# GpSimd's SBUF-only instructions made to wait for VectorE's in the attention of an attention, MoE and MLP kernel

## The chip, the cores and the metric

One core of a Trainium2 chip runs the whole program in one launch. The metric is the device time of that core in microseconds (us), the median of three runs. PE is TensorE (PEld its weight loads), DVE VectorE, ACT ScalarE, POOL GpSimd, SP SyncE. Each engine works through its own list of instructions in order; an instruction may wait on semaphores that others raise, and then everything behind it on its engine waits too.

## The reference

Three stages follow each other. Only the first is touched.

```python
q_pool = q.reshape(B, H, S // 2, 2, D).mean(axis=3)            # B, H, S, D = 4, 8, 1152, 64
scores = (1 / np.sqrt(D)) * (q_pool @ k.transpose(0, 1, 3, 2)) # 576 queries x 1152 keys a head
attn = np.exp(scores - scores.max(-1, keepdims=True))
x = (attn / (attn.sum(-1, keepdims=True) + 1e-9)) @ v          # -> 2304 tokens x 512
x = moe(x)                            # top-1 of 8 experts, 512 -> 1024 -> 512, gated
out = relu(x @ w_in) ** 2 @ w_out     # 512 -> 2048 -> 512
```

## The kernel before, in words

The 32 heads are worked off as 16 pairs, 18 steps a pair. In a step one tile of 128 keys x 512 queries goes through: PE makes the scores `st` (L397), ACT the exponential `p` in f32 (L415), whose upper half read as bf16 is the high part of the probability; the low part `pl` = `p` - high, f16, is made by `low` (L425); PE then multiplies both parts with the values (`pv`, L462). Three tiles a pair (`p32x`, `plx`) hold the odd queries. `low` goes to VectorE for the tiles in the plan's list `low` (every second one) and to GpSimd for the rest and for the odd tiles.

For the pair after that, the same steps carry the preparation: `prep` loads keys, queries and values and splits them in two f16 parts (`split`: ACT makes the high part, L239, VectorE the low one, L241; the outputs are `krow`, `qr2` and `vx`), GpSimd adds neighbouring queries (`qsum`, L261, output `qs`), which ACT then splits first; transposing DMAs turn them. The running maximum of the scores is found ahead of time in `smax_red`: ACT's `rd` from one PSUM tile (L364), then VectorE's fused maximum over another PSUM tile and `rd` (L367, with a short read of the accumulator behind it), block maxima `mc` (L358), and a small `tensor_scalar` from the maxima `mx` into `qr2` (L376). `kdiff` (L318) makes differences of keys on VectorE. `evac` scales the outputs out of PSUM (L484 to L503). `Route` classes the tokens of a finished batch between the steps; its `lo` (L691) makes `xhl`.

What stands where is set by `run`: each job has a step and a rank in it, and the lists of all engines are written in that order (ranks: load 0, scores 1, exponential 2, `smax_red` 2.2, 4.6 and 6.5, `kdiff` 4.4, `prep` 5, `low` 6, route 7). The schedule is manual: the order written is the order run, and semaphores are added only where data or a buffer calls for one. A VectorE instruction here is called **SBUF-only** when all it reads and writes lies in SBUF; L367, L358 and the evacuations read PSUM.

Of the kernel before, what the change touches and what calls it, by code (L numbers as in the profile page):

```python
# [14 lines left out]
ALU = mybir.AluOpType  # L15
# [121 lines left out]
class Attention:  # L137
# [3 lines left out]
    def __init__(self, ctx, kctx, pctx, tc, q, k, v, xbp, xdone):  # L141
        self.tc, self.nc = tc, tc.nc
        self.q, self.k, self.v = q, k, v
        self.xdone = xdone
        B, H, S, D = q.shape
        assert S == 1152 and D == 64
        self.B, self.H = B, H
        self.HP = H // 2
        self.NP = B * self.HP
        pool = lambda n, b, **kw: ctx.enter_context(tc.tile_pool(name=n, bufs=b, **kw))  # L150
        keys = lambda n, b: kctx.enter_context(tc.tile_pool(name=n, bufs=b, side="right"))
        self.raw = keys("raw", 1)
        self.row = keys("row", 1)
        self.t1p = keys("t1", 3)
        self.r2p = pool("r2", 2)
        self.pp = pool("pp", 22)
        self.sm = pool("sm", 2)
        self.xbp = xbp
        self.per = pool("per", 1)
        psum = lambda n, b: pctx.enter_context(tc.tile_pool(name=n, bufs=b, space=PSUM))  # L160
        self.ps_t = psum("ps_t", 2)
        self.ps_m = psum("ps_m", 4)
        self.ps_v = psum("ps_v", 2)
        self.t2 = [self.per.tile([128, 18, 128], F16, name=f"t2_{i}") for i in range(2)]
        self.qr2 = [self.per.tile([128, 9, 128], F16, name=f"qr2_{i}") for i in range(2)]
        self.vx = [self.per.tile([128, 18, 130], F16, name=f"vx_{i}") for i in range(2)]
        self.st = {}
        self.routes = {}

    def init(self):  # L170
        V = self.nc.gpsimd
        for t in self.qr2[::-1]:
            V.memset(t, 0.0)
        for t in self.vx:
            V.memset(t[:, :, 64:65], 1.0)
        for t in self.t2:
            V.memset(t[64:65], MROW)

        zero = self.qr2[1].rearrange("p a b -> p (a b)")[:, 0:512]
        ps = self.ps_m.tile([128, 512], F32, tag="sm", name="warm")  # L180
        for _ in range(WARM):
            self.nc.tensor.matmul(
                out=ps, lhsT=zero[:, 0:128], rhs=zero, start=True, stop=True,
                skip_group_check=True,
            )

    def load(self, h):
# [37 lines left out]
    def prep(self, h, n):  # L225
        nc = self.nc
        s = self.st[h]
        if n == 0:
            s["krow"] = self.row.tile([128, 18, 128], F16, tag="krow", name="krow")
            s["qrow"] = self.row.tile([128, 9, 128], F16, tag="qrow", name="qrow")  # L230
            s["qs"] = self.row.tile([128, 9, 64], F32, tag="qs", name="qs")
            s["t1"] = self.t1p.tile([128, 18, 128], F16, tag="t1", name="t1")
            s["r1"] = self.t1p.tile([128, 9, 128], F16, tag="r1", name="r1")
            s["qr2"] = self.qr2[h % 2]
            s["vx"] = self.vx[h % 2]

        def split(src, hi, lo, sc, what):
            if what == 0:
                nc.scalar.activation(out=hi, in_=src, func=ACTF.Copy, scale=sc)  # L239
            else:  # L240
                nc.vector.scalar_tensor_tensor(  # L241
                    out=lo, in0=src, scalar=sc, in1=hi, op0=ALU.mult, op1=ALU.subtract
                )

        def k_(i, what):
            kr = s["kr"][:, i].rearrange("p (c d) -> p c d", d=64)
            row = s["krow"][:, 9 * i:9 * i + 9]
            split(kr, row[:, :, 64:128], row[:, :, 0:64], KS, what)

        def v_(i, what):  # L250
            vr = s["vr"][:, i].rearrange("p (c d) -> p c d", d=64)
            vx = s["vx"][:, 9 * i:9 * i + 9]
            split(vr, vx[:, :, 0:64], vx[:, :, 65:129], VS, what)

        def kt(c=slice(0, 18)):
            nc.sync.dma_start_transpose(
                out=s["t1"][:, c], in_=s["krow"][:, c].rearrange("p a b -> p (a b)")
            )

        def qsum(c=slice(0, 9)):  # L260
            (nc.gpsimd if h else nc.vector).tensor_tensor(  # L261
                out=s["qs"][:, c], in0=s["qr"][:, c, 0], in1=s["qr"][:, c, 1], op=ALU.add
            )

        def q_(what, c=slice(0, 9)):
            split(s["qs"][:, c], s["qrow"][:, c, 0:64], s["qr2"][:, c, 0:64], QS, what)

        def qdup(c=slice(0, 9)):
            hi, dup = s["qrow"][:, c, 0:64], s["qrow"][:, c, 64:128]
            if h:  # L270
                nc.scalar.activation(out=dup, in_=hi, func=ACTF.Copy)
            else:
                nc.vector.tensor_copy(out=dup, in_=hi)
            nc.sync.dma_start_transpose(
                out=s["r1"][:, c], in_=s["qrow"][:, c].rearrange("p a b -> p (a b)")
            )

        if not h and n < 7:

            c, k = (slice(0, 4), slice(0, 9)) if n < 4 else (slice(4, 9), slice(9, 18))  # L280
            if n == 6:
                q_(1)
            elif n % 4 == 0:
                qsum(c)
                q_(0, c)
                k_(n // 4, 0)
            elif n % 4 == 1:
                qdup(c)
                k_(n // 4, 1)
                kt(k)  # L290
            return
        [
            lambda: (qsum(), k_(0, 0)),
            lambda: k_(0, 1),
            lambda: k_(1, 0),
            lambda: (k_(1, 1), kt()),
            lambda: q_(0),
            lambda: qdup(),
            lambda: q_(1),
            lambda: v_(0, 0),  # L300
            lambda: v_(0, 1),
            lambda: v_(1, 0),
            lambda: v_(1, 1),
        ][n]()
# [7 lines left out]
    def kdiff(self, h, a=slice(0, 2)):  # L312

        s = self.st[h]
        if a.start == 0:
            s["kd"] = self.sm.tile([128, 2, 512], BF16, tag="m24", name="kd")
        t1 = s["t1"].rearrange("p (a c) b -> p a (c b)", a=2)
        self.nc.vector.tensor_tensor(  # L318
            out=s["kd"][:, a], in0=t1[:, a, 512:1024], in1=t1[:, a, 0:512], op=ALU.subtract
        )  # L320

    def smax(self, h, i):

# [96 lines left out]
    def low(self, h, i, dve):  # L420
        nc = self.nc
        s = self.st[h]
        eng = nc.vector if dve else nc.gpsimd
        pl = s["pl", i] = self.ptile(i, "pl", F16)
        eng.tensor_tensor(out=pl, in0=s.pop(("p32", i)), in1=s["ph", i], op=ALU.subtract)  # L425

    GROUPS = (
        ((0, 0), (0, 1), (0, 2)),
# [1127 lines left out]
class First:  # L1556
# [97 lines left out]
    def psum(self, t, f2):  # L1654
        ps = self.att.ps_m.tile([128, 512], F32, tag="sm", name="h0")
        self.h[t, f2] = ps[:, 0:2 * T].rearrange("p (a b) -> p a b", a=2)
        return self.h[t, f2]
# [45 lines left out]
def build(tc, q, k, v, emb, tau, w1, w2, w_in, w_out, consts, at, out):  # L1703
    nc = tc.nc
    pool = lambda c, n, b, **kw: c.enter_context(tc.tile_pool(name=n, bufs=b, **kw))
    with ExitStack() as ctx, tc.manual_schedule():
# [3 lines left out]
        with ExitStack() as actx:  # L1710
# [18 lines left out]
            att = Attention(actx, kctx, pctx, tc, q, k, v, xbp, xdone)  # L1729
            first = First(moe, att)  # L1730
            init, zeros = moe.init(rb), moe.zeros()
            last = 18 * (att.NP - 1)
            extra = [(i, lambda: next(init, None)) for i in PLAN["init"]]
            extra += [(i, lambda: next(zeros, None)) for i in PLAN["zeros"]]

# [139 lines left out]
```

## Time and profile before

| | us |
|---|---|
| median of three runs (1138.07 to 1147.18) | 1143.66 |
| the profiled execution's own time | 1142.18 |
| its span, first to last instruction | 1140.4 |
| mean granted clock of TensorE, as a share of 2.4 GHz | 0.967 |
| busy: PE, DVE, ACT, POOL | 1061.1, 722.1, 527.5, 531.3 |

The attention takes the first 450 us or so of the span. A busy PE in such a profile has modelled ends, so 93% busy is not 93% of its peak. A group's row gives count, busy time, mean duration in ns, and the engine's idle time just before its instructions with what ended it.

### The profile page before, as it was taken

Reading aid. Unit: us, or ns where it says so; the run is one execution under the profiler, and the core shown is the slowest. Engines: PE = TensorE matmul, PEld = TensorE weight load, DVE = VectorE, ACT = ScalarE, POOL = GpSimd, SP = SyncE. Lnnn points to the kernel's source line nnn. Section 1 sums busy time; section 2 is a strip of 40 time slices with the busy share of each in tenths; the row PEclk is TensorE's granted clock in tenths of the full one; section 3 lists DMA queues with packets and bytes.
Section 4 is the critical chain, followed back from the end, with each engine's and each line's share of the span. In section 5 each row is a group of like instructions: output and inputs, shape, how many; then the busy total and the mean of one; then the engine's idle time right before and its main releaser. Section 6 shows DMA issues by size and latency. Waiting matters only on the chain. (4 is left out here: it accounts for less than half of the span.)

```text
span 1140.4 us, 28256 instructions
## 1 busy us (share of the span) xinstructions
PE 1061.1 (93%) x11340; PEld 724.6 (64%) x11340; DVE 722.1 (63%) x1374; ACT 527.5 (46%) x998; POOL 531.3 (47%) x454
## 2 busy tenths in 40 slices
PE   6898899999999889999899799998799999999996
PEld 2465556656665566999899699975454454555543
DVE  6999989999998988866664548848850021211200
ACT  5776677678876756423222335534440031322200
POOL 4765655566765646522443426637760142322301
PEclk9999989999998989999999899999899999999998
DMA  8665765656766537569579699223310000000000
GB/s 221 146 141 155 192 160 123 145 141 143 155 135 139 110 67 194 142 190 226 103 96 231 140 228 272 55 52 104 108 38 19 29 10 20 10 10 20 10 19 28
DMA packets 170830, 128.98 MB, mean 113 GB/s; under 512 B 129816, under 2 KB 134040, under 8 KB 170672
## 3 DMA queue, kind: packets, MB, share of 16 engines
q1 hardware_dynamic: 164912, 109.09, 41.8%
q0 software_dynamic: 5760, 17.85, 5.2%
q8 instruction: 91, 1.49, 0.6%
q14 instruction: 67, 0.55, 0.2%
HBM read 74.69 MB, written 12.60 MB: 77 GB/s over the span
## 5 line engine op out<-in xcount | busy, mean ns | idle before, releaser
L425 POOL TENSOR_TENSOR pl<-p 128x512 f16<-128x512 f32 x144 | 176.8, 1233 | 155.1 <-ACT p L415 150.1
L415 ACT ACTIVATE p<-st 128x512 f32<-128x512 f32 x288 | 169.4, 598 | 81.1 <-PE st L397 78.2
L397 PE MATMUL st<-r,t 128*128 128x64 f16 (+3 forms) x1152 | 198.8, 294 | 8.3 <-ACT p L415 7.7
L1446 PE MATMUL a<-yT,win 128*128 128x384 f16 x1056 | 178.6, 333 | 11.3 <-DVE r L1452 8.8
L462 PEld LDWEIGHTS <-p 128*128 128x128 bf16 x2304 | 135.9, 99 | 59.6 <-issue 6.7
L1446 PEld LDWEIGHTS <-win 128*128 128x128 f16 (+1 forms) x1152 | 114.4, 99 | 89.7 <-issue 18.7
L462 PE MATMUL pv<-vx,p 128*128 128x65 f16 x2250 | 159.9, 197 | 2.4 <-DVE xb L503 2.4
L1531 PE MATMUL o<-wo,gh 128*128 128x512 f16 (+1 forms) x528 | 157.0, 379 | 0.0
L462 PE MATMUL pv<-vx,pl 128*128 128x65 f16 x1125 | 144.7, 194 | 0.0
L425 DVE TENSOR_TENSOR pl<-p 128x512 f16<-128x512 f32 x144 | 141.5, 984 | 3.5 <-ACT p L415 3.5
L1451 ACT ACTIVATE r<-a 128x384 f32<-128x384 f32 x88 | 42.6, 486 | 185.6 <-PE a L1446 138.6
L1398 PEld LDWEIGHTS <-ws 128*128 128x128 f16 (+1 forms) x1344 | 114.0, 100 | 15.7 <-POOLq L1218 9.5
L1538 DVE TENSOR_SCALAR ot<-o,cms 128x512 f32<-128x512 f32 x18 | 13.5, 750 | 171.4 <-PE o L1531 171.4
L1398 PE MATMUL fst<-hl,ws 128*128 128x192 f16 x448 | 112.0, 250 | 9.9 <-DVE hl L1282 9.9
L1398 PE MATMUL fst<-hh,ws 128*128 128x192 f16 x896 | 117.0, 250 | 3.3 <-POOLq L1218 3.3
L397 PEld LDWEIGHTS <-t 128*128 128x128 f16 (+1 forms) x1152 | 75.4, 99 | 69.8 <-issue 33.7
L367 DVE CUSTOM_DVE_ANT_0 rd<-sm,rd,mc 128x512 bf16<-128x512 f32 x144 | 106.2, 742 | 18.3 <-PE sm L341 6.5
L1466 POOL TENSOR_TENSOR gl<-r,gh 128x384 f16<-128x384 f32 x88 | 87.7, 1006 | 64.0 <-ACT gh L1465 63.8
L1386 PE MATMUL fsm<-x,ws 128*128 128x192 f16 x1344 | 113.2, 246 | 0.0
L1386 PEld LDWEIGHTS <-ws 128*128 128x128 f16 (+1 forms) x1344 | 111.1, 98 | 0.4
L462 PEld LDWEIGHTS <-pl 128*128 128x128 f16 x1152 | 111.1, 101 | 0.0
L1452 DVE SCALAR_TENSOR_TENSOR r<-a,r 128x384 f32<-128x384 f32 x88 | 48.9, 555 | 85.5 <-ACT r L1451 85.2
(250 smaller groups left out, 1727.2 us busy)
## 6 DMA issues: line engine op xcount, KB each, us to landing
stg<-in_moe_w SPq DMA_DIRECT2D x24, 1024.0 KB, 7.9
vr<-in_v SPq DMA_DIRECT2D x16, 576.0 KB, 4.5
kr<-in_k SPq DMA_DIRECT2D x15, 576.0 KB, 5.5
fill<-in_moe_w_in POOLq DMA_DIRECT2D x16, 512.0 KB, 7.4
g<-in_moe_w_out SPq DMA_DIRECT2D x16, 512.0 KB, 3.4
qr<-in_q SPq DMA_DIRECT2D x15, 512.0 KB, 5.3
t<-t SPq DMA_DIRECT2D x16, 288.0 KB, 3.8
xs<-tmp SPq DMA_DIRECT2D x16, 192.0 KB, 3.9
```

The costliest lines, as they stand in the source:

```text
L367: nc.vector.tensor_tensor_reduce(out=rd, in0=ps, in1=rd, scale=1.0, scalar=mc[:, slots:slots + 1], op0=ALU.add, op1=ALU.max, accum_out=mx[ ...
L397: nc.tensor.matmul(out=st[:, j * n:j * n + n], lhsT=lhs[0:kk, m, :], rhs=r[0:kk, c0:c0 + n], start=first, stop=(kk == 65), skip_group_chec ...
L415: nc.scalar.activation(out=p, in_=st[:, 0:p.shape[1]], func=ACTF.Exp, scale=SCALE)
L425: eng.tensor_tensor(out=pl, in0=s.pop(("p32", i)), in1=s["ph", i], op=ALU.subtract)
L462: nc.tensor.matmul(out=o[:, 0:vn], lhsT=s[p, i][:, cs:cs + w], rhs=vx[:, 9 * a_ + c, v0:v0 + vn], start=(u == 0 and p == "ph" and v0 == 0) ...
L1386: self.nc.tensor.matmul(out=ps[:, f, 0:w], lhsT=w1(wh, f2)[:, fs], rhs=x[:, 4 * xh + k, 0:w], start=(f == 0 and m == 0), stop=(m == 11), s ...
L1398: self.nc.tensor.matmul(out=yp[m // 2][:, m % 2, 0:w], lhsT=w2(wh, f)[:, ds], rhs=h(l, f), start=(f == i == m % 2 == 0), stop=(f == 7 and ...
L1446: nc.tensor.matmul(out=ps, lhsT=half(self.win[wh][:, k, fs], wh), rhs=self.yT[yh][:, k, c0], start=(m == 0), stop=(m == 11),)
L1451: nc.scalar.activation(out=r, in_=ps, func=ACTF.Relu)
L1452: nc.vector.scalar_tensor_tensor(out=r, in0=ps, scalar=0.0, in1=r, op0=ALU.max, op1=ALU.mult)
L1466: self.nc.gpsimd.tensor_tensor(out=lo, in0=g, in1=hi, op=ALU.subtract)
L1531: nc.tensor.matmul(out=ps, lhsT=at(l, f)[:, rs], rhs=half(wout[wh][:, f], wh), start=(m == 0), stop=(m == 47),)
```

## The change

Two helpers are added. `vec` remembers the VectorE instruction it is given; `gps` makes the GpSimd instruction it is given depend on the one remembered last. Given to `vec` are the low splits (L241), `kdiff` (L318), `low` on VectorE, and the first pair's `qsum`; given to `gps` are `low` on GpSimd and the other pairs' `qsum`. No instruction is moved, added to VectorE or taken away. VectorE waits for nothing new.

```diff
+        self.port = None
...
+    def vec(self, ins):
+        self.port = ins.ins
+
+    def gps(self, ins):
+        if self.port is not None:
+            self.tc.add_manual_dep(
+                ins.ins, self.port.name,
+                mybir.DependencyInfo(mybir.DependencyClass.Sync, mybir.DependencyReason.DATA),
+                reason="port",
             )
...
-                nc.vector.scalar_tensor_tensor(
+                self.vec(nc.vector.scalar_tensor_tensor(
                     out=lo, in0=src, scalar=sc, in1=hi, op0=ALU.mult, op1=ALU.subtract
-                )
+                ))
...
-            (nc.gpsimd if h else nc.vector).tensor_tensor(
+            (self.gps if h else self.vec)((nc.gpsimd if h else nc.vector).tensor_tensor(
                 out=s["qs"][:, c], in0=s["qr"][:, c, 0], in1=s["qr"][:, c, 1], op=ALU.add
-            )
+            ))
...
-        self.nc.vector.tensor_tensor(
+        self.vec(self.nc.vector.tensor_tensor(
             out=s["kd"][:, a], in0=t1[:, a, 512:1024], in1=t1[:, a, 0:512], op=ALU.subtract
-        )
+        ))
...
-        eng.tensor_tensor(out=pl, in0=s.pop(("p32", i)), in1=s["ph", i], op=ALU.subtract)
+        ins = eng.tensor_tensor(out=pl, in0=s.pop(("p32", i)), in1=s["ph", i], op=ALU.subtract)
+        (self.vec if dve else self.gps)(ins)
```

GpSimd's list some 125 us into the span, before, with the semaphores that each row waits for (Activation is ACT, DMAHW a DMA queue; 15 lines are added ahead, so L425 reads L440 in the changed program):

```order
L261 TENSOR_TENSOR qs_2455<-qr_2065 128x576 [waits DMAHW5_49,DMAHW6_49,DMAHW4_49,DVE_49]
L425 TENSOR_TENSOR pl_2460<-p32_2382 128x512 [waits Activation_49]
L425 TENSOR_TENSOR pl_2513<-p32_2465 128x512 [waits Activation_49]
L425 TENSOR_TENSOR plx_2515<-p32x_2467 128x384 [waits Activation_49]
L425 TENSOR_TENSOR pl_2568<-p32_2522 128x512 [waits Activation_49]
L425 TENSOR_TENSOR pl_2636<-p32_2573 128x512 [waits Activation_49,Pool_49]
L425 TENSOR_TENSOR pl_2718<-p32_2643 128x512 [waits Activation_49,Pool_49]
```

The same place in the changed program:

```order
L276 TENSOR_TENSOR qs_2455<-qr_2065 128x576 [waits DMAHW5_49,DMAHW6_49,DMAHW4_49,Pool_49]
L440 TENSOR_TENSOR pl_2460<-p32_2382 128x512 [waits Activation_49]
L440 TENSOR_TENSOR pl_2513<-p32_2465 128x512 [waits DVE_49,Activation_49]
L440 TENSOR_TENSOR plx_2515<-p32x_2467 128x384 [waits Activation_49]
L440 TENSOR_TENSOR pl_2568<-p32_2522 128x512 [waits DVE_49,Activation_49]
L440 TENSOR_TENSOR pl_2636<-p32_2573 128x512 [waits DVE_49,Activation_49,Pool_49]
L440 TENSOR_TENSOR pl_2718<-p32_2643 128x512 [waits DVE_49,Activation_49,Pool_49]
```

The order is the same; a wait for VectorE has come to the first of each group that stands behind one VectorE instruction (`plx_2515` needs none of its own, since it runs behind `pl_2513`).

VectorE's list in the changed program, the stretch that these rows wait in (`pl_2513` and `plx_2515` wait for `pl_2486`, `pl_2568` for `pl_2541`, `pl_2636` for `pl_2596`; the two ISA rows are L367 and its read):

```order
L440 TENSOR_TENSOR pl_2486<-p32_2422 128x512
L382 ISA rd_2493,mx_2224<-sm_2510,rd_2493,mc_2225 128x512
L382 ISA mx_2224 128x1
L256 SCALAR_TENSOR_TENSOR krow_2453<-kr_2064,krow_2453 128x9x64
L440 TENSOR_TENSOR pl_2541<-p32_2491 128x512
L382 ISA rd_2548,mx_2224<-sm_2565,rd_2548,mc_2225 128x512
L382 ISA mx_2224 128x1
L440 TENSOR_TENSOR pl_2596<-p32_2546 128x512
L382 ISA rd_2604,mx_2224<-sm_2594,rd_2604,mc_2225 128x512
L382 ISA mx_2224 128x1
```

Nothing has moved here either; what a GpSimd instruction meets on VectorE once its wait is over is the row behind the one it waits for.

## Rows read from the trace of the kernel before

**Rows 1.** Page, part 2: VectorE's busy tenths in 40 slices of the span.
```profile
DVE  6999989999998988866664548848850021211200
```
**Rows 2.** Busy time by stretch: engine busy (count), granted clock, DMA share, GB/s.
```profile
100.00:140.00 40.00, 35.03 (x523) 22.54 (x522) 39.67 (x91) 27.04 (x50) 20.93 (x18) 1.00 0.70 176
...
180.00:220.00 40.00, 38.19 (x627) 25.66 (x625) 39.72 (x88) 32.69 (x61) 25.15 (x21) 1.00 0.68 144
...
340.00:380.00 40.00, 37.26 (x534) 23.45 (x531) 34.34 (x76) 28.58 (x59) 25.70 (x25) 0.87 0.49 119
```
**Rows 3.** Who waited for whom, 30 to 445 us: total, times, longest.
```profile
POOL pl L425 <- ACT p L415: 142.3, 91, 5.0
...
PE sm L341 <- DVE mx L367: 9.9, 13, 2.2
...
DVE pl L425 <- ACT p L415: 1.9, 2, 1.3
```
**Rows 4.** Groups by shape, 0 to 690 us, VectorE: count, busy, mean ns.
```profile
L425 DVE TENSOR_TENSOR pl<-p 128x512 f16<-128x512 f32 x144 | 141.5, 984 | 3.5 <-ACT p L415 3.5
...
L241 DVE SCALAR_TENSOR_TENSOR vx<-vr,vx 128x576 f16<-128x576 f32 x32 | 32.7, 1023 | 0.0
L241 DVE SCALAR_TENSOR_TENSOR krow<-kr,krow 128x576 f16<-128x576 f32 x32 | 32.6, 1020 | 2.0 <-ACT krow L239 2.0
...
L691 DVE SCALAR_TENSOR_TENSOR xhl<-xb,sc,xhl 128x512 f16<-128x512 f32 x16 | 15.3, 959 | 0.8 <-ACT xhl L686 0.8
L241 DVE SCALAR_TENSOR_TENSOR qr<-qs,qrow 128x576 f16<-128x576 f32 x16 | 14.1, 883 | 0.0
...
L376 DVE TENSOR_SCALAR qr<-mx 128x4 f16<-128x4 f32 x16 | 5.2, 324 | 0.1
```
**Rows 5.** Instructions of single lines: count, duration in ns min/median/max.
```profile
L425 DVE TENSOR_TENSOR pl<-p x144: 670/689/3285, 30.6 to 456.2; 128x512 f16<-128x512 f32 x144
...
L241 DVE SCALAR_TENSOR_TENSOR qr<-qs,qrow x15: 746/748/1517, 23.4 to 383.3; 128x576 f16<-128x576 f32 x15
...
L691 DVE SCALAR_TENSOR_TENSOR xhl<-xb,sc,xhl x16: 723/751/1536, 173.5 to 473.5; 128x512 f16<-128x512 f32 x16
...
L376 DVE TENSOR_SCALAR qr<-mx x32: 145/178/1393, 14.2 to 415.6; 128x4 f16<-128x4 f32 x16, 128x5 f16<-128x5 f32 x16
...
L425 POOL TENSOR_TENSOR pl<-p x144: 1029/1124/2016, 23.7 to 454.2; 128x512 f16<-128x512 f32 x144
L425 POOL TENSOR_TENSOR plx<-p32x x47: 818/1270/1434, 36.0 to 449.6; 128x384 f16<-128x384 f32 x47
```
**Rows 6.** Timeline, GpSimd, then VectorE, at a meeting: start us, duration us.
```profile
106.65 1.28 POOL L425 TENSOR_TENSOR pl<-p 128x512 f16<-128x512 f32 x1 [1.21 <-ACT p L415]
...
106.95 1.53 DVE L425 TENSOR_TENSOR pl<-p 128x512 f16<-128x512 f32 x1
108.40 0.14 DVE L930 TENSOR_TENSOR nt__1763<-nt__1763,nh 8x1 f32<-8x1 f32 x1
```
**Rows 7.** Timeline: GpSimd's `pl_2568`, then VectorE from `pl_2541` on.
```profile
130.48 1.04 POOL L425 TENSOR_TENSOR pl<-p 128x512 f16<-128x512 f32 x1 [0.73 <-ACT p L415]
...
134.25 0.68 DVE L425 TENSOR_TENSOR pl<-p 128x512 f16<-128x512 f32 x1
134.85 0.74 DVE L367 CUSTOM_DVE_ANT_0 rd<-sm,rd,mc 128x512 bf16<-128x512 f32 x1
...
135.52 1.11 DVE L425 TENSOR_TENSOR pl<-p 128x512 f16<-128x512 f32 x1
```
**Rows 8.** Timeline: the first `qsum` on GpSimd and the VectorE row that released it.
```profile
17.04 0.75 DVE L241 SCALAR_TENSOR_TENSOR krow<-kr,krow 128x576 f16<-128x576 f32 x1
...
17.79 1.39 POOL L261 TENSOR_TENSOR qs<-qr 128x576 f32<-128x576 f32 x1 [10.68 <-DVE krow L241]
```
**Rows 9.** Timeline: VectorE's `pl_2402`, which `qs_2455` will wait for; ACT's use of it.
```profile
128.21 0.85 DVE L425 TENSOR_TENSOR pl<-p 128x512 f16<-128x512 f32 x1
...
131.37 0.68 ACT L239 ACTIVATE qrow<-qs 128x576 f16<-128x576 f32 x1
```

More of the change, by code (lines that the diff above doesn't have):

```diff
@@ L184, in init @@
                 skip_group_check=True,
+            )
+    def vec(self, ins):
[6 more added lines that the diff above has]
+                reason="port",
             )
```

## The prediction

> **What bounds the kernel now.** The page's slices come first: VectorE stands at nine tenths or more in most slices of the attention and falls behind it [rows 1]. The stretches say when: at full clock VectorE is busy 39.67 and 39.72 of 40 us while PE has 5.0 and 1.8 us left; in a stretch that holds some time at half clock (0.87 on average) VectorE falls to 34.34 [rows 2]. So the attention goes at VectorE's pace, but for its half-clock stretches, where PE sets it. The waits agree: VectorE waited for `p` 1.9 us in all, GpSimd 142.3 us, and PE for VectorE's maxima 9.9 us [rows 3]. VectorE runs late, with its inputs ready; GpSimd runs ahead of it.
>
> What VectorE loses stands in its own rows. `low` takes 0.689 us in the median and 0.984 us on average; likewise the splits, 0.746 against 0.883 to 1.023, `xhl`, 0.723 against 0.959, and the small L376, 0.145 against 0.324 [rows 4, 5]. One meeting shows how: GpSimd's `low` runs from 106.65 to 107.93, VectorE's begins at 106.95 and takes 1.53 us, 0.55 of them after GpSimd is done [rows 6]. Two such instructions don't run beside each other; the later one waits. VectorE's next one starts at 108.40, 1.45 us after this one and not 0.60 (its usual spacing, 134.25 to 134.85 [rows 7]): 0.85 us lost for 0.98 us of overlap, so **loss = overlap less 0.13**, since part of an instruction's start is hidden behind the wait.
>
> The sum of what is lost (count x (mean less undisturbed), [rows 4, 5]): `pl` 144 x 0.295 = 42.5; `vx` 32 x 0.277 = 8.9; `krow` 32 x 0.274 = 8.8; `qr` 16 x 0.137 = 2.2; `xhl` 16 x 0.236 = 3.8; L376 16 x 0.179 = 2.9. **69 us** of VectorE's time, on the path wherever VectorE sets the pace. Some 3 us of it are longer holds (the maximum of `pl` is 3.285) that no single GpSimd `low` explains; they stay.
>
> **The change, part by part.** *The wait comes last.* `pl_2568` starts at 130.48; `pl_2541`, which it will wait for, ends at 134.93 [rows 7]: 4.45 us later. GpSimd will start when VectorE lets it and no longer when ACT does. From VectorE's end to GpSimd's start nothing is lost: 17.04 + 0.75 = 17.79 [rows 8]. But VectorE's next instruction starts 0.08 us before that end (134.85 against 134.93 [rows 7]). So an undisturbed `low` of GpSimd, 1.03 us [rows 5], ends 1.11 us after the start of VectorE's next instruction.
>
> *What it meets there* decides the gain. VectorE's list in the changed program has 143 places that a GpSimd group waits for; I sort them by what stands behind.
> - 39 places: VectorE does maxima and evacuations out of PSUM until GpSimd is done. Loss 0.
> - 84 places: the next SBUF-only instruction (or L376) stands behind one L367, which takes 0.67 us to its successor (134.85 to 135.52 [rows 7]). Overlap 1.11 - 0.67 = 0.44, loss 0.31 each: 26 us.
> - In 27 of these 84 a second GpSimd instruction waits in the group, mostly a `plx` of 0.82 us [rows 5], and VectorE's next but one is SBUF-only too: 0.82 - 0.13 = 0.69 more, 19 us.
> - 20 places: an SBUF-only instruction stands right behind. It starts ahead of GpSimd's and loses nothing; in 4 of them the one after it loses about 0.9: 4 us.
>
> Sum 49, with the 3 of longer holds **52 us against 69: VectorE gains 17 us.** Unknown is whether L376 (22 of the 84) gets by after GpSimd's first instruction or is held through two; held through two it loses 0.8 more, 17 us in all, and nothing is gained. From below, if L376 slips in between as its median of 0.178 says it mostly does, its 7 us go and the gain is 24. I take 17, which the undisturbed rows give.
>
> *What of it reaches the end.* About a tenth of the attention runs at half clock, where VectorE has slack [rows 2]: 15 us are left. PE has 1.8 to 5.0 us of each 40 to give, 17 to 46 us over the 370 us at full clock, so it can follow, but not without waits of its own in the tighter stretches. I take two thirds, **10 us**; the ends are 0 and 17. The stages behind the attention, which the change doesn't touch, move forward with its end.
>
> *What the wait costs.* GpSimd is idle more than 142 us [rows 3], and its own time costs nothing. Queued behind the waiting instruction are more `low`, `qsum` and the issues of the token scatters. `pl` is read by PE steps later, so lateness of 4 us is mostly covered; where a `plx` or the last tile comes late I count 1 us. `qsum` has less cover: `pl_2402` ends at 129.06, then come a `plx` (0.82) and `qs_2455` (1.39 [rows 8]), at 131.27 at the earliest; ACT takes it at 131.37 [rows 9]. This place has 0.1 us left; it is the price of the third rival.
>
> The sum against the profiled execution: 1142.2 - 10 + 1 = **1133 us**. That execution is 1.5 us under the median of the runs, 1143.66. About 1%, 11.4 us, is what a measurement here can tell from no change.
>
> **Rivals.** *All of it arrives* (0.18). For it: the 99% of VectorE at full clock [rows 2], and L376's median. Then 17 to 24 us go: 1118 to 1126.
>
> *The losses only change places* (0.24). The GpSimd instruction now starts right behind a VectorE one, and in 84 of 143 places VectorE comes to an SBUF-only instruction again before GpSimd is done; VectorE, which bounds, still waits for GpSimd, which doesn't. If an overlap costs in full, without the 0.13 back, the loss is 84 x 0.44 + 27 x 0.82 + 4 x 1.03 + 3 = 66 against 69; with L376 held through two it is the same or worse. The time is then 1138 to 1146. Beside this: the Trainium skill, "SBUF — State Buffer", section "Who interferes with whom", says that a VectorE instruction with two SBUF inputs and a GpSimd one that reads SBUF take a shared port as an exclusive lock, that the first to issue holds it for the whole instruction, and that issue order decides who blocks. By that rule the sum would be the full overlap, 1142.2 - 2 = about 1140; the meeting [rows 6] agrees with the lock but shows 0.13 us less lost than the overlap, and by that I go. What the same rule says against the change is that it orders one side alone: VectorE's next instruction still blocks.
>
> *ACT stands behind a late `qsum`* (0.14), slower than before. ACT's list is in order; if `qs` comes late, the exponentials behind L239 wait, PE runs out of its two score tiles, and VectorE gets its maxima late. Price: where VectorE's own SBUF-only instructions slip in between the `plx`, `qsum` and `pl` of a group, each puts off the next by 0.67, so `qs` ends up to 1.3 us after ACT wants it; over 14 pairs that is 18 us, and with nothing gained on VectorE the time is 1155 to 1161. It decides where `qsum` ends later than ACT reaches L239 in most pairs, not in the one or two that have 0.1 us. Against it: ACT has 7 us and more of idle time in each 40 [rows 2] to take up single late places.
>
> That the change doesn't do what it says, because the wait never comes last, is out: VectorE is 4 us behind [rows 7].
>
> **How the numbers follow.** The forecast, 1126 to 1140, has 0.44. The predicted time is its middle. Faster by over 1% (under 1132.2) takes the first rival and 0.20 of the forecast: 0.38. Within 1% takes 0.24 of the forecast, the second rival, and 0.03 of the third: 0.51. Slower by over 1% is the rest of the third: 0.11. The range leaves out the lower end of the first rival and the upper end of the third: 1120 to 1152. The forecast's own range is 1126 to 1140.
>
> **What would show it.** Right: GpSimd's idle time before L425 is ended by VectorE and no longer by ACT; GpSimd's `low` falls to about 1.05 us in the median; VectorE's `pl` falls to 0.85 to 0.9 on average, `krow` and `vx` to under 0.95, while L376 rises; 4 to 12 us less from the first `low` to the last. Wrong: VectorE's `pl` stays at 0.98, which would be the second rival; ACT waits for `qs` over 10 us in all, which would be the third; VectorE's idle time in the full-clock stretches rises by as much as its busy time falls, which would say that PE or ACT was as near to being the bound.

## The result and the profile after

| | before | changed | ratio, 95% interval |
|---|---|---|---|
| median beside each other, 4 runs each, us | 1142.72 | 1130.65 | 0.9898 [0.9855, 0.9942] |
| the same once more, 13 and 10 runs | 1144.77 | 1133.33 | 0.9902 [0.9864, 0.994] |
| profiled execution, us | 1142.18 | 1129.53 | |

The change makes the kernel 1% faster, 11 to 12 us. A single execution says less: runs of one kernel spread over up to 20 us (of the kernel before from 1132.01 to 1151.91 in one set), and a profile shows one of them. Medians are of all runs; ratios leave out runs more than 1.5% above the fastest of their kernel.

First the whole attention as one stretch, from 24 us to the end of the last `low`, in each kernel's trace. The columns are those of [rows 2]: length, then busy time (count) of PE, PEld, DVE, ACT and POOL, mean granted clock, DMA share, GB/s. The kernel before:
```profile
24.00:456.94 432.94, 398.30 (x5985) 256.90 (x5982) 401.62 (x875) 319.39 (x602) 269.84 (x223) 0.95 0.63 145
```
The changed kernel, that stretch and those of [rows 2]:
```profile
24.00:444.98 420.98, 392.46 (x5961) 255.18 (x5987) 395.78 (x875) 319.32 (x603) 246.73 (x223) 0.96 0.66 149
...
100.00:140.00 40.00, 36.33 (x532) 23.14 (x531) 38.75 (x93) 28.17 (x52) 22.39 (x20) 0.96 0.77 185
...
180.00:220.00 40.00, 38.00 (x616) 25.34 (x615) 39.75 (x87) 30.63 (x57) 22.43 (x20) 0.99 0.69 138
...
340.00:380.00 40.00, 36.81 (x578) 23.80 (x578) 38.45 (x85) 31.58 (x63) 25.19 (x23) 1.00 0.70 149
```
The attention is 11.96 us shorter, which is nearly all of the 12.65 between the two profiled executions; the stages behind it only start earlier. VectorE is busy 5.8 us less and idle 6.1 us less (31.3 and 25.2). So half of the gain is time that VectorE no longer loses, and half is idle time, which the prediction had no term for. At full clock VectorE still sets the pace (39.75 of 40); the stretch at 340 us had a half-clock stretch before (0.87) and has none now.

Who waited for whom in the changed kernel, 30 to 445 us, as [rows 3]:
```profile
POOL pl L440 <- DVE pl L440: 82.4, 57, 4.3
...
POOL pl L440 <- DVE kd L333: 19.8, 9, 2.9
...
POOL pl L440 <- ACT p L430: 16.4, 8, 3.4
...
PE sm L356 <- DVE mx L382: 3.5, 7, 0.9
...
ACT qrow L254 <- POOL qs L276: 0.8, 1, 0.8
```
GpSimd now waits for VectorE and little for ACT (16.4 us for `p`, 142.3 before); PE's waits for the maxima fell from 9.9 to 3.5; ACT waited once for `qs`.

The groups of the changed kernel that answer to [rows 4], GpSimd's `low` ahead of them:
```profile
L440 POOL TENSOR_TENSOR pl<-p 128x512 f16<-128x512 f32 x144 | 157.5, 1095 | 168.3 <-DVE pl L440 82.4 <-DVE kd L333 19.8 <-ACT p L430 16.4
...
L440 DVE TENSOR_TENSOR pl<-p 128x512 f16<-128x512 f32 x144 | 130.4, 907 | 0.4 <-ACT p L430 0.3
...
L256 DVE SCALAR_TENSOR_TENSOR krow<-kr,krow 128x576 f16<-128x576 f32 x32 | 36.2, 1132 | 2.3 <-ACT krow L254 2.3
...
L256 DVE SCALAR_TENSOR_TENSOR vx<-vr,vx 128x576 f16<-128x576 f32 x32 | 26.8, 837 | 0.7 <-ACT vx L254 0.7
...
L707 DVE SCALAR_TENSOR_TENSOR xhl<-xb,sc,xhl 128x512 f16<-128x512 f32 x16 | 15.9, 998 | 0.8 <-ACT xhl L702 0.8
L256 DVE SCALAR_TENSOR_TENSOR qr<-qs,qrow 128x576 f16<-128x576 f32 x16 | 13.0, 810 | 0.0
L391 DVE TENSOR_SCALAR qr<-mx 128x4 f16<-128x4 f32 x16 | 12.6, 785 | 0.1
```
By the prediction's own sum the losses are `pl` 31.4, `vx` 2.9, `krow` 12.4, `qr` 1.0, `xhl` 4.4 and L376 (L391 here) 10.2: **62 us against 69**. `pl` and `vx` fell by 17 us together; `krow` and L376 took 11 of them back.

Where they went, in one place of the changed kernel. Timeline, GpSimd's rows first, then VectorE's:
```profile
258.35 1.04 POOL L440 TENSOR_TENSOR pl<-p 128x512 f16<-128x512 f32 x1 [0.72 <-DVE pl L440]
259.35 1.27 POOL L440 TENSOR_TENSOR plx<-p32x 128x384 f16<-128x384 f32 x1
260.59 1.40 POOL L276 TENSOR_TENSOR qs<-qr 128x576 f32<-128x576 f32 x1
...
257.01 1.17 DVE L440 TENSOR_TENSOR pl<-p 128x512 f16<-128x512 f32 x1
258.17 0.75 DVE L382 CUSTOM_DVE_ANT_0 rd<-sm,rd,mc 128x512 bf16<-128x512 f32 x1
...
258.85 1.09 DVE L440 TENSOR_TENSOR pl<-p 128x512 f16<-128x512 f32 x1
...
260.81 1.22 DVE L391 TENSOR_SCALAR qr<-mx 128x4 f16<-128x4 f32 x1
```
VectorE's `pl` ends at 258.18 and GpSimd's starts at 258.35: the hand-over takes 0.17 us (in 113 such starts of this trace it is 0.17 in the median). VectorE's next `pl` comes at 258.85, overlaps 0.54 us and takes 0.40 more than 0.689: the overlap less 0.14, where 0.13 was forecast. This is one of the milder places: in the 26 of this trace where such a `pl` stands behind one L382, the overlap is 0.61 us and the loss 0.47 in the median. Then each engine waits for the other in turn: `plx` takes 1.27 and not 0.82, since VectorE's `pl` runs until 259.94, and L391 is held to the end of `qsum` (its own end at 262.03, that of `qsum` at 261.99).

### The profile page after: what moved, and what is told of

It reads as the page before. It is cut to its first block, busy times and chain, and to the rows that moved or that the text cites. A ratio compares the mean times of both kernels' runs of the same rounds, so it can differ in the third digit from the quotient of the medians.

```text
span 1127.8 us, 28266 instructions
## 1 busy us (share of the span) xinstructions
PE 1055.1 (94%) x11297; PEld 723.6 (64%) x11340; DVE 712.4 (63%) x1374; ACT 527.0 (47%) x998; POOL 507.6 (45%) x454
## 5 line engine op out<-in xcount | busy, mean ns | idle before, releaser
L440 POOL TENSOR_TENSOR pl<-p 128x512 f16<-128x512 f32 x144 | 157.5, 1095 | 168.3 <-DVE pl L440 82.4
L1547 PE MATMUL o<-wo,gh 128*128 128x512 f16 (+1 forms) x513 | 153.8, 379 | 0.0
L440 DVE TENSOR_TENSOR pl<-p 128x512 f16<-128x512 f32 x144 | 130.4, 907 | 0.4 <-ACT p L430 0.3
L382 DVE CUSTOM_DVE_ANT_0 rd<-sm,rd,mc 128x512 bf16<-128x512 f32 x144 | 106.6, 743 | 15.9 <-ACT p L430 4.0
```

What stands on the lines that cost most here:

```text
L382: nc.vector.tensor_tensor_reduce(out=rd, in0=ps, in1=rd, scale=1.0, scalar=mc[:, slots:slots + 1], op0=ALU.add, op1=ALU.max, accum_out=mx[ ...
L440: ins = eng.tensor_tensor(out=pl, in0=s.pop(("p32", i)), in1=s["ph", i], op=ALU.subtract)
L1547: nc.tensor.matmul(out=ps, lhsT=at(l, f)[:, rs], rhs=half(wout[wh][:, f], wh), start=(m == 0), stop=(m == 47),)
```

## The experiments

The stretch of each trace from 24 us to the end of its last `low`, read as above (times in us; idle is length less busy). The kernel before, run beside them, had medians of 1143.47 (e1 to e4), 1144.77 (e5 to e8) and 1144.38 (e9 to e12); from one of these sets to another, compare ratios:

| run | median | ratio to the kernel before | length | VectorE busy | idle | clock |
|---|---|---|---|---|---|---|
| changed | 1130.65 | 0.9898 [0.9855, 0.9942] | 420.98 | 395.78 | 25.2 | 0.96 |
| e7, changed again | 1133.33 | 0.9902 [0.9864, 0.994] | 417.95 | 394.95 | 23.0 | 0.98 |
| e1, `low` only | 1126.75 | 0.9876 [0.9803, 0.995] | 419.46 | 395.94 | 23.5 | 0.97 |
| e2, wait for L367 | 1156.9 | 1.0133 [1.0058, 1.0208] | 448.80 | 424.95 | 23.9 | 0.94 |
| e3, memset, before | 1103.63 | 0.9677 [0.9606, 0.9749] | 395.06 | 335.06 | 60.0 | 0.99 |
| e4, memset, changed | 1100.05 | 0.9646 [0.9577, 0.9715] | 393.31 | 333.57 | 59.7 | 0.99 |
| e5, L376 on GpSimd | 1127.39 | 0.9871 [0.9816, 0.9925] | 417.91 | 393.04 | 24.9 | 0.97 |
| e6, e5 with `low` only | 1126.79 | 0.9862 [0.9797, 0.9927] | 416.06 | 393.96 | 22.1 | 0.97 |
| e8, halves | 1124.18 | 0.982 [0.9766, 0.9875] | 418.86 | 386.25 | 32.6 | 0.96 |
| e10, halves and e5 | 1126.7 | 0.9807 [0.9781, 0.9833] | 419.01 | 379.33 | 39.7 | 0.96 |
| e11, halves, no wait | 1132.93 | 0.9884 [0.9851, 0.9916] | 426.16 | 401.38 | 24.8 | 0.96 |
| e12, quarters | 1148.97 | 0.9991 [0.9961, 1.0022] | 443.13 | 385.60 | 57.5 | 0.92 |
| e9, before again | 1144.32 | 0.9976 [0.9932, 1.002] | 443.07 | 402.21 | 40.9 | 0.92 |

**The other phase (e2).** `vec` is called on L367 instead of on the SBUF-only instructions:

```diff
-            nc.vector.tensor_tensor_reduce(
+            self.vec(nc.vector.tensor_tensor_reduce(
```


> The changed kernel, but GpSimd's low and qsum wait for the last L367 that was issued ahead (which reads PSUM), no longer for the last SBUF-only instruction. GpSimd is about as late as in the changed kernel (within 1 us), only its phase against VectorE is another one: in about half of the places an SBUF-only instruction of VectorE stands right behind the awaited one. Theory A (phase decides): VectorE's pl is back at 0.95 to 1.0 us on average, the losses at 65 to 80 us, and the time at 1138 to 1148. Theory C (the lateness is what helps: GpSimd no longer runs ahead, its losses fall on it and not on VectorE, or the PE runs smoother): pl about 0.9 and the time as the changed kernel's, 1127 to 1133.

GpSimd waits about as long for L367 as for `pl` in the changed kernel. Groups of e2:
```profile
L442 POOL TENSOR_TENSOR pl<-p 128x512 f16<-128x512 f32 x144 | 185.1, 1294 | 160.2 <-DVE mx L384 85.2 <-DVE rs L503 30.4 <-ACT p L432 27.6
L442 DVE TENSOR_TENSOR pl<-p 128x512 f16<-128x512 f32 x144 | 140.2, 976 | 4.8 <-ACT p L432 4.8
...
L393 DVE TENSOR_SCALAR qr<-mx 128x4 f16<-128x4 f32 x16 | 17.6, 1097 | 0.1
```
Idle before `low` is 160.2 us (168.3 in the changed kernel), but `pl` is back at 0.976, L376 at 1.097, VectorE is busy 23 us longer than before the change, and the kernel is slower than it was by 1.3%: 1156.9 us, above theory A's 1138 to 1148. The 23 us are not in `pl`; by the rows of the two traces L376 takes 12.4 us more than in the kernel before, `kd` 4.9, `xhl` 4.3 and `vx` 3.5. So it isn't lateness that helps. What VectorE does while GpSimd runs decides.

**Meetings with `low` taken out (e3, e4).** GpSimd's `low` becomes a memset, which only writes and takes half as long. It waits for the same exponential; the low part of these tiles is left out. `qsum` stays as it is.

```diff
-        eng.tensor_tensor(out=pl, in0=s.pop(("p32", i)), in1=s["ph", i], op=ALU.subtract)
+        if dve:
+            eng.tensor_tensor(out=pl, in0=s.pop(("p32", i)), in1=s["ph", i], op=ALU.subtract)
+        else:
+            ins = eng.memset(pl, 0.0)
+            self.tc.add_manual_dep(
+                ins.ins, s["ex", i].name,
...
```


> The kernel before, with each low on GpSimd replaced by a memset of the same tile at the same place (it waits for the same exponential; the low part of those tiles is left out). It bounds what all meetings cost. If a GpSimd instruction that only writes SBUF does not hold VectorE: pl falls from 0.984 to 0.70 us, the low splits to 0.75 to 0.85, some 50 to 60 of the 69 us lost on VectorE go. Theory A (VectorE's time is the time, about two thirds of what it gains arrive): 33 to 40 us less, 1103 to 1110. Rival (PE is nearly the bound, so little of it arrives): at most 15 us less, 1128 to 1135. If a write alone holds VectorE as well: pl stays above 0.9 and the time above 1130.

> The changed kernel, waits and all, with the same memset in the place of GpSimd's low (the low part of those tiles is left out). Against the memset in the kernel before, it has the waits and no meetings to avoid, so the difference is the price of the waits alone. Forecast: 0 to 2 us more than the memset without waits. Rival: the lateness of 4 us costs 5 us or more (PE waits for pl or plx, ACT for qs). Other rival: the lateness itself is a gain (5 us less or more), which would mean that the gain of the change does not come from meetings.

Groups of e4, GpSimd then VectorE:
```profile
L443 POOL MEMSET pl<- 128x512 f16 x144 | 75.7, 526 | 248.5 <-DVE pl L441 125.7 <-DVE kd L333 27.9 <-ACT vx L254 15.2
...
L441 DVE TENSOR_TENSOR pl<-p 128x512 f16<-128x512 f32 x144 | 98.9, 688 | 2.6 <-ACT p L430 2.6
...
L391 DVE TENSOR_SCALAR qr<-mx 128x4 f16<-128x4 f32 x16 | 12.5, 784 | 0.1
```
A GpSimd instruction that only writes doesn't hold a VectorE instruction with two inputs from SBUF: `pl` is at its undisturbed 0.688. The Trainium skill, "SBUF — State Buffer", section "Who interferes with whom", says this of the shared port; the row agrees. The small `tensor_scalar` (L376, here L391) is another matter. Timeline of e3, GpSimd, then VectorE:
```profile
171.64 0.52 POOL L428 MEMSET pl<- 128x512 f16 x1 [2.01 <-ACT p L415]
...
171.86 0.34 DVE L376 TENSOR_SCALAR qr<-mx 128x4 f16<-128x4 f32 x1
```
The same of e4:
```profile
143.71 1.41 POOL L276 TENSOR_TENSOR qs<-qr 128x576 f32<-128x576 f32 x1 [1.07 <-issue]
145.06 0.53 POOL L443 MEMSET pl<- 128x512 f16 x1
...
144.71 0.91 DVE L391 TENSOR_SCALAR qr<-mx 128x4 f16<-128x4 f32 x1
```
In e3 it meets only memsets and takes 0.34 us, not 0.145, to 0.04 us after the end of the one that was running (172.16). In e4 it is held through `qsum` and the memset behind it (145.59), to 145.62. So a write holds this instruction as well.

In e3 VectorE has 66.6 us less to do and 39.8 us of time go, the upper end of theory A's 33 to 40: 0.6 us per us, until PE sets the pace (382.34 of 395.06 us busy). This is nearly the whole price of the meetings; the change takes back somewhat over a quarter.

The waits alone cost nothing that shows: e4 is 3.6 us under e3, inside both intervals, where 0 to 2 us more were forecast. All four runs of e4 lie below all four of e3, so a small gain is not excluded. But the attention accounts for 1.75 us of the 5.1 between the two profiled spans (1102.2 and 1097.1); the rest lies behind it, where no wait was added.

**qsum's wait (e1, e6) and a second profile (e7).**

```diff
-            (self.gps if h else self.vec)((nc.gpsimd if h else nc.vector).tensor_tensor(
+            ins = (nc.gpsimd if h else nc.vector).tensor_tensor(
...
+            if not h:
+                self.vec(ins)
```


> The changed kernel, with qsum let go: only GpSimd's low waits for VectorE. Theory A (the 12 us come from fewer and shorter meetings of low with VectorE's SBUF-only work): 14 qsum of 175 waiting groups are a small part, so the time stays at 1129 to 1134. Theory B (qsum's wait has a price, since ACT needs qs at once; the third rival in a small size): 2 to 6 us less than the changed kernel, 1124 to 1129, and ACT's wait for qs, 0.8 us there, goes. If qsum's wait was itself a gain (it met krow, whose mean rose to 1.132 us in the changed kernel): krow rises further and the time is 1133 to 1138.

> As the one before, and qsum does not wait. If qsum's wait costs about 4 us by itself (1126.75 against 1130.65, from two sets of runs), this is 3 to 5 us under the one before. If that difference was only half-clock stretches that came or stayed away (one of 10.2 us more in the changed kernel's profile than without qsum's wait, worth 2.4 us in its pair of heads), the two are within 2 us of each other.

> The changed kernel once more, for a second profile and runs beside the others. Theory A: the losses of VectorE (about 66 us) and most pairs of heads repeat to 0.3 us; the time is 1127 to 1132. If the half-clock stretches are chance, this profile has 28 to 45 us of them at other places than the first (37.5 us), and the last low ends 2.5 to 3 us earlier or later for each stretch of 10 us that is missing or added.

e1 lies 4 to 7 us under the two medians of the changed kernel, in theory B's range, but the ratios' intervals overlap, VectorE is busy the same 395.9 us, and with L376 moved the two forms are equal (1126.79 and 1127.39). So `qsum`'s wait has no price that these runs show. In e7 the median came out at 1133.33, just over the 1127 to 1132 expected; the second profile of the changed kernel repeats VectorE's busy time to 0.8 us:
```profile
24.00:441.95 417.95, 389.08 (x5985) 253.05 (x5984) 394.95 (x878) 319.51 (x604) 247.79 (x223) 0.98 0.67 151
```
Its attention is 3.0 us shorter than that of the first profile, with a mean clock of 0.98 against 0.96.

**L376 on GpSimd (e5).**

```diff
-                nc.vector.tensor_scalar(
+                nc.gpsimd.tensor_scalar(
                     out=s["qr2"][:, sl, 64], in0=mx[:, sl], scalar1=-1.0 / MROW,
```


> The changed kernel with L376, the small tensor_scalar from the maxima into qr2, moved from VectorE to GpSimd, at the same place of the order. On VectorE it took 17.6 us in the changed kernel (16 x 0.785 + 16 x 0.31), most of it held by GpSimd. Theory A (VectorE's lost time is the time, at about 0.65 us per us, as the memset in the kernel before measured: 40 us of time for some 61 us lost): 9 to 12 us less than the changed kernel, 1118 to 1122. Rival (the hold goes over to the next SBUF-only instruction, krow or pl, or the transposing DMA behind L376 now comes late and PE or ACT wait for it): within 3 us of the changed kernel, 1127 to 1133.

Groups of e5:
```profile
L440 DVE TENSOR_TENSOR pl<-p 128x512 f16<-128x512 f32 x144 | 144.7, 1007 | 0.0
```
L376's 17.6 us left VectorE, and `pl` rose by 14.3 us (130.4 to 144.7): the rival. VectorE is busy 2 to 3 us less, and the time is 3 to 6 us lower, under theory A's 9 to 12. What one instruction is spared, the next SBUF-only one pays. One thing is not kept apart here: the moved instructions take GpSimd 11.4 us (267.09 us busy and not 246.73), so part of `pl`'s rise can be meetings with them.

**Smaller pieces (e8, e10, e11, e12).** GpSimd's `low` in two instructions, both with the wait; in four in e12; in two, and in the kernel before, so without a wait, in e11; in two and with L376 on GpSimd in e10. The edit of e8:

```diff
+        for c in ((slice(0, n),) if dve else (slice(0, n // 2), slice(n // 2, n))):
+            ins = eng.tensor_tensor(out=pl[:, c], in0=p32[:, c], in1=ph[:, c], op=ALU.subtract)
+            (self.vec if dve else self.gps)(ins)
```


> The changed kernel with each low on GpSimd (plx too) issued as two instructions of half the columns, both with the same wait. By the rows (1.03 us for 512 columns, 0.82 for 384) a half takes about 0.6 us, so the first half ends before VectorE comes back from one L367 (0.67 us). Theory A (a VectorE instruction waits for the one GpSimd instruction that is in flight when it comes, and gets in between two): a hold is at most 0.55 us, the losses fall by 10 to 25 us and the time by 5 to 15, to 1116 to 1126. Rival D (VectorE stays held while GpSimd has its next instruction ready, as krow was held 3.09 us through qsum and low in the changed kernel): the pair takes 1.2 us and not 1.03, the losses rise by 10 us or more, and the time is 1133 to 1142.

> The kernel before, without any wait, with GpSimd's low in halves. If the size of the GpSimd instruction is what decides (a hold ends with it, VectorE gets in between two halves), the halves alone give most of it: 10 to 16 us under the kernel before, 1128 to 1134, and the wait adds 4 to 10 on top. If VectorE is not let in between two halves that follow each other without a wait: no gain, 1140 to 1150. If the halves alone come to the time of halves with the wait, 1122 to 1127, the wait is not needed.

> The changed kernel with GpSimd's low in halves and L376 on GpSimd, both at once. Theory A (lost time of VectorE is what is left of the GpSimd instruction in flight): L376's 13 us on VectorE go, and less of its hold passes on to pl and krow than with whole lows, so 3 to 6 us under the halves alone: 1117 to 1122. Rival (what is taken from one VectorE instruction is paid by the next, as pl rose by 13 us when L376 went): within 2 us of the halves alone, 1122 to 1127.

> The changed kernel with each low on GpSimd in four instructions, with the same wait. From 1.03, 0.82 and 0.61 us for 512, 384 and 256 columns a quarter takes about 0.4 us. Theory A: a hold is at most 0.35 us, but a tile now takes 1.6 us of GpSimd, so VectorE meets it more often: losses 45 to 58 us, and the time 1116 to 1124. Rival (four pieces mean that GpSimd's work is spread over so much time that every SBUF-only instruction of VectorE meets one, or pl comes too late for PE): losses above 60 us or PE's waits for pl up from 2 us, and the time 1126 or more.

The attention of e8, then of e12:
```profile
24.00:442.86 418.86, 394.82 (x5985) 255.49 (x5984) 386.25 (x875) 319.06 (x602) 308.13 (x414) 0.96 0.67 151
```
```profile
24.00:467.13 443.13, 406.08 (x5984) 260.56 (x5983) 385.60 (x876) 320.16 (x603) 406.39 (x796) 0.92 0.62 143
```
Groups of e8, VectorE:
```profile
L443 DVE TENSOR_TENSOR pl<-p 128x512 f16<-128x512 f32 x144 | 131.2, 913 | 2.3 <-ACT p L430 2.3
...
L256 DVE SCALAR_TENSOR_TENSOR krow<-kr,krow 128x576 f16<-128x576 f32 x32 | 28.9, 904 | 2.1 <-ACT krow L254 2.1
```
With halves VectorE is busy 9 us less than in the changed kernel, GpSimd 60 us more. `pl` gains nothing (131.2 us, 130.4 before the cut); `krow` does (28.9, 36.2) and L376 (9.7, 12.6). GpSimd's half now waits (0.760 us in the mean against 0.612 in the median), as it does where VectorE gets in between two halves. Halves with the wait are the fastest full kernels here (e8 and, with L376 moved, e10), e8 6 to 9 us under the changed one. Without the wait (e11) they bring as much as the wait alone, and the expected time, though VectorE's busy time does not fall. Taking L376 away as well (e10) gives VectorE 7 us more and no time beyond the noise: theory A fails there. PE is busy 395.01 of 419.01 us.

The quarters show where this ends. VectorE is busy no longer than with halves, but GpSimd is busy 406 of 443 us and what it makes comes late. Waits of e12, 30 to 445 us:
```profile
PE st L412 <- ACT p L430: 15.7, 16, 3.7
ACT qrow L254 <- POOL qs L276: 11.6, 8, 3.9
...
PE pv L481 <- POOL plx L443: 4.2, 5, 1.3
```
ACT waits for `qs` (11.6 us, 0.8 in the changed kernel), PE for ACT (15.7, 7.0): this is the prediction's third rival, here with a busy GpSimd and not only a late one.

**The kernel before again (e9).** Nothing is edited.

> The kernel before once more, for a second profile. The first had 44.4 us at half clock in the attention, the two of the changed kernel 37.5 and 27.3. If fewer half-clock stretches are a part of the change's effect (an attention that VectorE holds less lets PE run with fewer pauses), this profile has 38 us or more of them, and the last low ends at 453 us or later (444.98 and 441.95 in the changed kernel). If they are chance, it may have 27 to 37, and the last low ends near 450. VectorE's losses repeat at 70 to 74 us either way.

Its attention, in the same columns:
```profile
24.00:467.07 443.07, 409.15 (x5985) 262.07 (x5985) 402.21 (x876) 320.96 (x603) 266.25 (x223) 0.92 0.61 142
```
VectorE's busy time repeats to 0.6 us, and yet the attention is 10.1 us longer, all of it idle time, at a mean clock of 0.92 against 0.95. This execution took 1149.94 us, the second longest of ten, so it fits the first line of the expectation without deciding it. What it does show is the scatter: two executions of one program differ by 10 us with half-clock stretches, and by 0.6 us in VectorE's busy time.

## Why the prediction came out right

**The bound and the mechanism: right.** VectorE loses its time to GpSimd's instructions, nearly all of it to `low`: with its reads gone 39.8 us go (e3). The wait comes last (GpSimd's idle time is now ended by VectorE), and lateness costs nothing that shows (e4), where 1 us was charged. `vx` fell to 0.837, and L376 rose, as said; `pl` at 0.907 is just over its 0.85 to 0.9; `krow` should have come under 0.95 and rose to 1.132. From the first `low` to the last 13.0 us went, just over the 4 to 12. That GpSimd's `low` fell to 1.04 us in the median, as forecast, was no sign: in the second profile of the kernel before it is 1.048.

**VectorE's gain of 17 us: mis-sized, it is 6 to 7** (5.8 and 6.7 in two profiles; 6.6 by the sum of losses). Three terms were too good. The hand-over was taken as nothing, from one row [rows 8], and is 0.17 us. That row showed no hand-over: in the changed kernel the same `qsum` starts 0.03 us before that `krow` ends (17.26 + 0.75 = 18.01), and the profile puts its wait down to the load of the queries:
```profile
17.98 1.39 POOL L276 TENSOR_TENSOR qs<-qr 128x576 f32<-128x576 f32 x1 [10.88 <-DMA qr<-in_q]
...
17.26 0.75 DVE L256 SCALAR_TENSOR_TENSOR krow<-kr,krow 128x576 f16<-128x576 f32 x1
```
So GpSimd ends that much later; the median place with a `pl` lost 0.47 where I had 0.31, and over 84 places that would be 13 us, an estimate. L376, left unknown, came out nearer to "held through": 0.64 us each where the sum had 0.31, 10.2 us lost against 2.9 before. And the long holds didn't stay as they were: two of `krow` in the kernel before (2.97 and 2.13 us) became four (3.09 twice and 2.16 twice). Together this is more than the 10 us by which the sum is off (62 against 52), so other terms came out smaller; which, is open. One of the long holds goes through `qsum` and `low`, which follow each other without a gap. Timeline of the changed kernel there:
```profile
364.16 1.42 POOL L276 TENSOR_TENSOR qs<-qr 128x576 f32<-128x576 f32 x1
365.54 1.04 POOL L440 TENSOR_TENSOR pl<-p 128x512 f16<-128x512 f32 x1
...
364.12 3.09 DVE L256 SCALAR_TENSOR_TENSOR krow<-kr,krow 128x576 f16<-128x576 f32 x1
```
**What reaches the end, 10 of 17: the ratio was about right for a large gain (0.6 in e3), and doesn't describe this one.** Here 11 to 12 us came from 6 to 7. The rest is idle time of VectorE, and the granted clock accounts for about as much. It is on record for every run: the ten runs of e7 have 0.970 in the mean, the 13 of the kernel before beside them 0.964; over all sets it is 0.970 in 14 runs against 0.964 in 51. Within either kernel's runs of that set a clock 0.01 higher goes with 7 to 9 us less, so the difference is worth some 5 us, an estimate. With VectorE's 6 to 7 that makes the 11 to 12, and a chance of two profiles against two it is not. Why the changed kernel is granted more isn't shown. That a VectorE that is held for less long at a time lets PE run with fewer pauses is an argument; e11 fits it, with 0.970 against 0.963 of the 21 runs beside it, 11 us faster at an unchanged busy time of VectorE. The clock is in e3's ratio of 0.6 too (0.980 against 0.967). So 1133 met the measured 1130.65 and 1133.33 by luck in the sizes, not in the mechanism: VectorE's gain was put too high, and a gain that the prediction had no term for made up for it.

**The rivals.** That all of it arrives is true of the 6 to 7 us, but its price was 17 to 24: VectorE never had that to give. That the losses only change places is half true: of 17 us that `pl` and `vx` gave up, `krow` and L376 took 11, and e5 shows the same passing on. The loss is still the overlap less 0.14 and not the whole of it; why a part comes back, no run shows. ACT behind a late `qsum` didn't happen here, and did in e12.

## What to carry to other kernels

When two engines shut each other out, a wait that sets which of them starts first helps only if the other then has work that doesn't collide for the whole length of the instruction let go: list what stands behind each awaited instruction, and add the hand-over to the length. Here, cutting the off-path engine's instruction in halves as well gained more than the wait alone, and cutting further lost it all, because that engine then ran out of time. Where runs of one program scatter by more than the gain, compare the bounding engine's busy time, which repeats, and beside it the clock granted in every run, which here goes with about half of the gain.

## What the runs showed of the hardware

- From the end of a VectorE instruction to the start of a GpSimd one that waits for it: 0.14 to 0.17 us in most of 113 places, not nothing.
- A 128x4 `tensor_scalar` from f32 to f16, one input from SBUF, 0.145 us undisturbed, is held to the end of a GpSimd `tensor_tensor` (1.22 us at 260.81) and of a GpSimd memset (0.34 us at 171.86 in e3). The same page and section of the Trainium skill count `tensor_scalar` among the operations that can take the shared port; the row agrees.
- A 128x512 memset takes GpSimd 0.526 us and doesn't hold VectorE's `pl`, which has two inputs from SBUF (0.688 us in e4).
- Between two GpSimd instructions without a gap VectorE mostly gets in (`pl` at 258.85, ahead of `plx`), but not always (`krow` at 364.12; L391 in e4, through `qsum` and a memset, at 144.71). What decides was not tried.
